# Fused attention, gated MLP and routed experts: turns tied to a place in PE's order, four weight slabs loaded early, the last expert's sums tile by tile, and a re-ordered last routing step

## The chip, the cores and the metric

One NeuronCore of one Trainium2 chip. The metric is device time in microseconds of one execution; the time before is 820.84 us, the median of three runs (818.26 to 821.02). All data are float32 in the reference. The kernel works in the chip's 32-bit matmul type with operands split into a high and a low part, and takes three products for each product of the reference.

## The reference, cut to what matters

```python
def reference(**kwargs):
    attn_out = _attn_ref(**attn_kwargs)              # 2 x 8 heads x 768 x 64, window 96, 8 global
    x = attn_out.transpose(0, 2, 1, 3).reshape(1536, 512)
    x = _moe_ref(x=x, **moe_kwargs)                  # rms norm, (silu(x w_gate) * (x w_val)) w_out, d_ff 1536
    return _moe2_ref(x=x, **moe2_kwargs)

def _moe2_ref(x, w_gate, w_noise, noise, w1, w2):    # 1536 tokens, 512 wide, 8 experts, d_ff 1024
    noisy = x @ w_gate + np.log1p(np.exp(x @ w_noise)) * noise
    top2 = the two largest of noisy per token
    top2_w = softmax over those two
    for e in range(E):
        for k in range(2):
            mask = top2[:, k] == e
            h = np.maximum(x[mask] @ w1[e], 0.0)
            out[mask] += top2_w[mask, k, None] * (h @ w2[e])
```

## The kernel before, in words

The program runs three stages one after another on PE: attention, the gated MLP, and the routed experts. A planner of the framework orders the instructions of each engine: it walks the program with estimated times and issues what it believes to be ready, in program order of priority. `follow(a, b)` (L269) adds an order without a semaphore: a stands behind b on its engine. Each engine then runs its list strictly in that order.

**The MLP** (L1009 to L1058) goes through visits (chunk of hidden blocks, first token tile, number of token tiles). A step f of a visit is `up` for the gate (L646, 12 products), `up` for the value (12 products), `hidden` (tanh, two DVE operations, the split into dh and dl) and the `down` of the step before (L672). The last six visits are of two token tiles each. When a visit of the last chunk ends, its tiles are stored to DRAM as x2d (L685), and `finish` (L999) calls `route` for them.

**Routing** (`route`, L718) transposes two token tiles, evacuates them (L729), forms the logits (L731) in a PSUM bank of tag "o", picks the top two on DVE, counts earlier tokens per expert with small products (L758 to L761), and gets a slot for each choice (sl, L789). The slots, cast to integers (si, L791), drive four scatters on POOL (L812) that write token number and weight into the list metad in DRAM. The two weights come from ed, w1_ (L793 to L800). After the third routing step the fullest expert so far is known (lead); it becomes units 0 and 1, with the first 256 and the other 256 slots of that expert. After the last step, DVE counts and sorts the other seven experts (order, L823 to L830), and SP reads them into registers (value_load, L1059).

**The last routing step** does not go through DRAM for unit 1: `late_slots` (L691) builds four one-hot rows (hot, L700) from sl, multiplies them on PE with late2, which holds a token number and the weight in three bf16 parts (L805 to L807), so that one set of eight products gives token number and weight of each slot. It adds them to the list that was fetched before (L708 to L716), clamps the numbers on POOL (ic, L862), and gathers.

**A unit** (`Unit`, L842) is up to 512 slots of one expert. `slots` fetches its list by an SP transfer (L853) and clamps it; `gather` (L871) brings 128 rows of x2d by an indirect DMA of POOL, 256 KB; `turn` (L881 to L884) transposes the rows on PE into a PSUM bank of tag "t" or "o" and splits them into gh (ACT) and gl (DVE). `run` (L893) goes over eight steps f: `up` (L907, 12 products), Relu and split (zh, zl; L911, L912), and `down` of the step before (L923 or L929). Units 2 to 6 take the transposed form of `down`; units 0, 1, 7 and 8 sum into one bank per tile of 128 slots (L929). After the last step the sums are weighted (L961, L964) and scattered to the output by POOL (L965). Unit 8, the last, has 368 slots, three tiles.

Weights come as slabs of 256 KB by SP (`moe2_weights`, L835 to L841): one w1 and one w2 slab for each f, eight f for each expert, into 19 shared buffers of tag "raw". Units 0 and 1 share theirs. The next unit's slots, gathers, turns and slabs are placed in the program by `side(f)` (L1067) of the unit that runs: fetch at f 0, gathers at f 1 and on, turns at the last f (for unit 1's run, of 4 tiles: f 4 to 7), slabs at each f. SP issues its queue in order.

## Time and profile before

| | before |
|---|---|
| median of 3 runs | 820.84 us (818.26 to 821.02) |
| profiled execution | 815.08 us, of which the span is 812.9 us |
| mean granted TensorE clock | 0.985 |
| PE busy in 420 to 440, 480 to 500, 500 to 520 us | 15.25, 16.74, 14.97 of 20.00 us each |
| DMA moved | 88.76 MB, mean 109 GB/s |

How to read it: the span runs from the first to the last event of the profiled execution. PE is the matmul engine, PEld its weight loads, DVE the vector engine, ACT the scalar engine, POOL the general engine that also issues indirect DMAs, SP the engine that issues the plain ones. A timeline row gives the start, the duration, engine, line, operation, output<-input and, in brackets, the idle time of that engine before it and what ended it. The granted clock is in parts of full speed (1.00 is 2.4 GHz, 0.50 is 1.2 GHz).

### The profile page before, as it was taken

What the parts mean: (1) busy time and instruction counts of PE and PEld (TensorE: products, weight loads), DVE (VectorE), ACT (ScalarE), POOL (GpSimd) and SP (SyncE); (2) the same over time, 40 slices, a digit from 0 to 9 for tenths busy, and PEclk for the clock granted to TensorE, in tenths of its full rate; (3) what the DMA queues carried; (4) which work ended last, traced back from release to release, by engine and by line L of the source; (5) the groups of instructions that cost most, each with busy time, mean ns of one, the idle gap of its engine ahead of it and who ended that gap; (6) DMA issues with size and microseconds to landing.
All of it is one profiled execution on the core that took longest, in us unless ns stands there. A gap on an engine that the chain in (4) does not pass through costs nothing. (4 is left out here: it accounts for less than half of the span.)

```text
span 812.9 us, 13827 instructions
## 1 busy us (share of the span) xinstructions
PE 778.2 (96%) x5041; PEld 696.2 (86%) x5041; DVE 459.6 (57%) x1053; ACT 362.6 (45%) x807; POOL 312.9 (38%) x353
## 2 busy tenths in 40 slices
PE   8999999999899999999997996999999999999993
PEld 5789999999788888899996985888999999999982
DVE  4489866667487887334453575533545454545541
ACT  5677656656443443123332463433333434344430
POOL 7437742232285565002421335342424343524311
PEclk9999999999999999999999999999999999999997
DMA  8465421260242330010108005973363728272010
GB/s 187 106 165 146 118 65 28 45 190 15 79 130 93 118 100 0 1 52 27 27 9 242 25 18 159 330 240 120 104 207 114 246 89 269 87 234 75 36 37 34
DMA packets 116838, 88.76 MB, mean 109 GB/s; under 512 B 49449, under 2 KB 100649, under 8 KB 116768
## 3 DMA queue, kind: packets, MB, share of 16 engines
q1 hardware_dynamic: 107920, 65.43, 28.7%
q0 software_dynamic: 7120, 19.27, 7.1%
q10 hardware_dynamic: 1728, 3.15, 1.3%
q8 instruction: 41, 0.67, 0.4%
q14 instruction: 29, 0.24, 0.1%
HBM read 75.18 MB, written 13.34 MB: 109 GB/s over the span
## 5 line engine op out<-in xcount | busy, mean ns | idle before, releaser
L907 PE MATMUL pz<-gh,sa 128*128 128x256 f32 (+7 forms) x576 | 157.6, 340 | 0.8 <-ACT gh L883 0.8
L907 PEld LDWEIGHTS pz<-gh,sa 128*128 128x128 f32 x576 | 104.2, 190 | 6.2 <-ACT gh L883 1.0
L907 PE MATMUL pz<-gl,sa 128*128 128x256 f32 (+7 forms) x288 | 97.8, 339 | 0.9 <-DVE gl L884 0.9
L672 PE MATMUL acc<-wo,dh 128*128 128x512 f32 x288 | 88.3, 400 | 0.8 <-ACT dh L658 0.8
L923 PE MATMUL ac<-zh,sb 128*128 128x480 f32 (+4 forms) x320 | 86.3, 364 | 0.0
L911 ACT ACTIVATE zh<-pz 128x256 fp32r<-128x256 f32 (+7 forms) x72 | 35.1, 487 | 110.0 <-PE pz L907 110.0
L912 DVE SCALAR_TENSOR_TENSOR zl<-pz,zh 128x256 fp32r<-128x256 f32 (+7 forms) x72 | 39.8, 553 | 75.1 <-ACT zh L911 74.8
L646 PE MATMUL pz<-xTh,wg 128*128 128x256 f32 x352 | 73.7, 288 | 1.2 <-ACT xTh L550 1.0
L646 PE MATMUL pz<-xTh,wv 128*128 128x256 f32 x352 | 73.9, 288 | 0.1
L628 ACT ACTIVATE sa<-wab 128x512 fp32r<-128x512 f32 x72 | 45.2, 629 | 57.9 <-PE ac L923 40.5
L632 DVE TENSOR_TENSOR sa<-wab,sa 128x512 fp32r<-128x512 f32 x51 | 36.6, 720 | 45.5 <-ACT sa L628 45.3
L646 PEld LDWEIGHTS pz<-xTh,wg 128*128 128x128 f32 x352 | 58.4, 192 | 3.5 <-ACT xTh L550 1.2
L923 PEld LDWEIGHTS ac<-zh,sb 128*128 128x128 f32 x320 | 57.9, 188 | 3.2
L672 PEld LDWEIGHTS acc<-wo,dh 128*128 128x128 f32 x288 | 51.3, 189 | 9.7 <-ACT dh L658 1.4
L646 PEld LDWEIGHTS pz<-xTh,wv 128*128 128x128 f32 x352 | 58.4, 192 | 0.8 <-ACT wv L599 0.5
L659 POOL TENSOR_TENSOR dl<-u,dh 128x256 fp32r<-128x256 f32 (+1 forms) x38 | 37.8, 996 | 53.0 <-ACT dh L658 44.7
L907 PEld LDWEIGHTS pz<-gl,sa 128*128 128x128 f32 x288 | 54.8, 190 | 3.8 <-DVE gl L884 1.1
L871 POOL DMA_INDIRECT xg<-x2d,ic x30 | 30.5, 1018 | 67.7 <-PE pg L881 61.3
L812 POOL DMA_INDIRECT metad<-meta,si x24 | 24.3, 1012 | 83.4 <-DVE si L791 77.3
L672 PE MATMUL acc<-wo,dl 128*128 128x512 f32 x144 | 53.0, 400 | 0.2 <-POOL dl L659 0.2
L923 PE MATMUL ac<-zl,sb 128*128 128x480 f32 (+4 forms) x160 | 52.9, 357 | 0.0
L632 DVE TENSOR_TENSOR sb<-wab,sb 128x512 fp32r<-128x512 f32 x67 | 47.1, 703 | 8.9 <-ACT sb L628 8.0
(268 smaller groups left out, 1872.4 us busy)
## 6 DMA issues: line engine op xcount, KB each, us to landing
wab<-in_moe_w_dram SPq DMA_DIRECT2D x128, 256.0 KB, 4.9
rg<-in_moe_w_gate_dram SPq DMA_DIRECT2D x12, 512.0 KB, 3.7
rv<-in_moe_w_val_dram SPq DMA_DIRECT2D x12, 512.0 KB, 3.7
ro<-in_moe_w_out_dram SPq DMA_DIRECT2D x12, 512.0 KB, 3.5
vn<-in_v_dram SPq DMA_DIRECT2D x12, 256.0 KB, 4.4
out_dram<-zero SPq DMA_DIRECT2D x1, 3072.0 KB, 12.8
x2d<-x ACTq DMA_DIRECT2D x12, 256.0 KB, 3.6
kn<-in_k_dram SPq DMA_DIRECT2D x11, 256.0 KB, 3.9
```

Of the source, the lines that this page charges most:

```text
L628: cp = nc.scalar.activation(wp[:, 0], src, AF.Copy)
L632: (nc.gpsimd if pool else nc.vector).tensor_sub(wp[:, 1], src, wp[:, 0].bitcast(F32))
L646: nc.tensor.matmul(pz, a[:, cs], x[:, tt:tt + nt, c, :], start=(n == 0), stop=(n == 3 * DC - 1))
L659: (nc.gpsimd if ci < len(CHUNKS) - 1 else nc.vector).tensor_sub(dl, u, dh.bitcast(F32))
L672: nc.tensor.matmul(acc[t], a[:, tt], w, start=(f == CHUNKS[ci][0] and n == 0), stop=(end and n == 2))
L812: st = nc.gpsimd.indirect_dma_start(out=metad, out_offset=bass.IndirectOffsetOnAxis(ap=si[:, t, kk:kk + 1], axis=0), in_=meta[:, G0[g] + t ...
L871: self.last = nc.gpsimd.indirect_dma_start(out=xg[:m], out_offset=None, in_=x2d[:self.rows], in_offset=bass.IndirectOffsetOnAxis(ap=self.i ...
L907: nc.tensor.matmul(pz[:, :cap], a[:, cs], x[:, c, :cap], start=(k == 0), stop=(k == 3 * DC - 1))
L911: nc.scalar.activation(dh[:, :cap], pz[:, :cap], AF.Relu)
L912: nc.vector.scalar_tensor_tensor(dl[:, :cap], pz[:, :cap], 0.0, dh[:, :cap].bitcast(F32), op0=ALU.max, op1=ALU.subtract)
L923: nc.tensor.matmul(acc[c][:, :cap], w[:, c * P:(c + 1) * P], a[:, :cap], start=(f == 0 and k == 0), stop=(f == FB2 - 1 and k == 2))
```

## The change

- **Turns.** Unit 0's two turns no longer stand in the middle of the visit before the last; each follows, by an order edge, the value products of the last visit's last two steps. Unit 1's two turns follow the eighth `up` of unit 0 (before: program places at f 6 and 7). Unit 2's four turns follow the seventh and eighth `up` of unit 1, two each (before: f 4 to 7, one each).
- **Early weights.** Behind the last routing step SP reads the first expert number alone and loads four of unit 2's eight pairs of slabs there; the rest follow at f 4 to 7 of unit 1's run. The other expert numbers are read one by one, at f 0 of the unit before.
- **Late routing.** `late_slots` is called as soon as sl is there. The one-hot rows are multiplied with the token-number column alone, the sum is clamped on DVE and the gathers are issued; si, ed and the running totals are ordered behind the one-hot rows; the split of the weights is ordered behind the written token numbers, and a second set of eight products then collects the weights. The second tile's transposes are evacuated by DVE. The third `up` of unit 0 is ordered behind the logits.
- **The last expert.** In unit 8 the last two `down` steps are held and done tile by tile, each tile's products in one chain of order edges; the third tile is summed in two halves of 256 columns, in two banks, in all steps, and weighted in two halves.

```diff
@@ -643,8 +643,9 @@
             for a, x in ((wh, xTh[g]), (wh, xTl[g]), (wl, xTh[g])):
-                nc.tensor.matmul(pz, a[:, cs], x[:, tt:tt + nt, c, :], start=(n == 0), stop=(n == 3 * DC - 1))
+                mm = nc.tensor.matmul(pz, a[:, cs], x[:, tt:tt + nt, c, :], start=(n == 0), stop=(n == 3 * DC - 1))
                 n += 1
+        return mm.ins
 
@@ -694,26 +695,33 @@
         h4 = pools["b"].tile([P, GS[-1], 2, 2 * P], BF16, name="hot", tag="raw", bufs=NRAW["b"])
+        idf = sb.tile([P, ns], F32, name="idf")
+        nc.vector.tensor_copy(idf, u.me[:, :ns, 0])
         hot = []
...
                 hot.append((h4[:, t, kk], late2[:, t, kk]))
-        idf = sb.tile([P, ns], F32, name="idf")
-        follow(nc.vector.tensor_copy(idf, u.me[:, :ns, 0]).ins, mark.ins)
         pl = lg[:, 256:256 + 4 * ns].rearrange("p (s c) -> p s c", s=ns)
-        for s in range(ns):
-            for i, (h, m) in enumerate(hot):
-                nc.tensor.matmul(pl[:, s], h[:, s * P:(s + 1) * P], m, start=(i == 0), stop=(i == len(hot) - 1))
+
+        def collect(cols):
+            for s in range(ns):
+                for i, (h, m) in enumerate(hot):
+                    nc.tensor.matmul(pl[:, s, cols], h[:, s * P:(s + 1) * P], m[:, cols], start=(i == 0), stop=(i == len(hot) - 1))
+        collect(slice(0, 1))
         nc.vector.tensor_add(idf, idf, pl[:, :, 0])
-        nc.vector.tensor_copy(u.me[:, :ns, 0], idf)
-        u.slots()
+        u.slots(idf)
         for s in range(ns):
             u.gather(s)
-        mf = u.me.bitcast(F32)
-        gain = sb.tile([P, ns], F32, name="gain")
-        nc.vector.tensor_reduce(gain, pl[:, :, 1:], axis=AX.X, op=ALU.add)
-        nc.vector.tensor_add(mf[:, :ns, 1], mf[:, :ns, 1], gain)
+        found = nc.vector.tensor_copy(u.me[:, :ns, 0], idf).ins
+
+        def gains():
+            collect(slice(1, 4))
+            mf = u.me.bitcast(F32)
+            gain = sb.tile([P, ns], F32, name="gain")
+            nc.vector.tensor_reduce(gain, pl[:, :, 1:], axis=AX.X, op=ALU.add)
+            nc.vector.tensor_add(mf[:, :ns, 1], mf[:, :ns, 1], gain)
+        return mark.ins, found, gains
 
@@ -726,10 +734,13 @@
             xt = sb.tile([P, DC, P], F32, name=f"x2T{ti}", tag="n2", bufs=N2)
-            nc.scalar.activation(xt, p3, AF.Copy)
+            if last and t % 2:
+                nc.vector.tensor_copy(xt, p3)
+            else:
+                nc.scalar.activation(xt, p3, AF.Copy)
             for c in range(DC):
-                nc.tensor.matmul(lg[:, t * 2 * E:(t + 1) * 2 * E], xt[:, c, :], wr[:, c, :], start=(c == 0),
-                                 stop=(c == DC - 1))
+                state["logits"] = nc.tensor.matmul(lg[:, t * 2 * E:(t + 1) * 2 * E], xt[:, c, :], wr[:, c, :], start=(c == 0),
+                                 stop=(c == DC - 1)).ins
         l4 = lg[:, :GT * 2 * E].rearrange("p (t e) -> p t e", t=GT)
@@ -759,8 +770,11 @@
             nc.tensor.matmul(pf[:, t], ones, selsum, start=False, stop=True)
-        for t in range(GT):
-            nc.vector.tensor_add(selsum, selsum, sel[:, t])
+        def total():
+            for t in range(GT):
+                nc.vector.tensor_add(selsum, selsum, sel[:, t])
+        if not last:
+            total()
         pe = small("pe", [E])
@@ -787,12 +801,18 @@
         nc.vector.tensor_reduce(sl.rearrange("p t k -> p (t k)"), oe.rearrange("p t k e -> p (t k) e"), axis=AX.X, op=ALU.add)
+        if last:
+            mark, found, gains = late_slots(sl, lg)
         si = small("si", [2], I32)
-        nc.vector.tensor_copy(si, sl)
+        cast = nc.vector.tensor_copy(si, sl).ins
         ed = small("ed", [1])
-        nc.vector.tensor_sub(ed, m8[:, :, 1:2], m8[:, :, 0:1])
+        w1_ = small("w1_", [1])
+        dif = nc.vector.tensor_sub(ed, m8[:, :, 1:2], m8[:, :, 0:1]).ins
+        if last:
+            follow(cast, mark)
+            follow(dif, mark)
+            total()
         nc.scalar.activation(ed, ed, AF.Exp)
-        w1_ = small("w1_", [1])
         nc.vector.tensor_scalar(w1_, ed, 1.0, 1e-9, op0=ALU.add, op1=ALU.add)
@@ -802,11 +822,13 @@
             for x in range(1, 4):
-                nc.vector.tensor_copy(late2[:, :, :, x], src)
+                part = nc.vector.tensor_copy(late2[:, :, :, x], src)
+                if x == 1:
+                    follow(part.ins, found)
                 if x < 3:
...
                 src = rest
-            late_slots(sl, lg)
+            gains()
         for t in range(GT):
@@ -853,13 +875,16 @@
 
-        def slots(self):
+        def slots(self, ids=None):
             n, ns = self.n, len(self.tiles)
...
             ic = sb.tile([P, NS], I32, name=f"ic{n}", tag="ic", bufs=3)
-            nc.gpsimd.tensor_scalar(ic[:, :ns], me[:, :ns, 0], self.rows - 1, None, op0=ALU.min)
+            if ids is not None:
+                nc.vector.tensor_scalar(ic[:, :ns], ids, float(self.rows - 1), None, op0=ALU.min)
+            else:
+                nc.gpsimd.tensor_scalar(ic[:, :ns], me[:, :ns, 0], self.rows - 1, None, op0=ALU.min)
             self.ic = ic
@@ -872,13 +897,15 @@
 
-        def turn(self, s):
+        def turn(self, s, behind=None):
             m = self.tiles[s][1]
...
             for c in range(DC):
-                nc.tensor.transpose(p3[:, c, :], xg[:m, c * P:(c + 1) * P], ident[:m, :m])
+                mm = nc.tensor.transpose(p3[:, c, :], xg[:m, c * P:(c + 1) * P], ident[:m, :m])
+                if behind is not None:
+                    follow(mm.ins, behind)
             ss = slice(s * P, s * P + m)
@@ -892,9 +919,14 @@
             n, cap, gh, gl = self.n, self.cap, self.gh, self.gl
+            ending = n == E and len(self.tiles) < 4
+
+            def cuts(s):
+
+                return (slice(0, DM // 2), slice(DM // 2, DM)) if ending and s + 1 == len(self.tiles) else (slice(0, DM),)
             wide = cap % P > 0 and cap > 2 * P and n < 8
             acc = [ps.tile([P, 512], F32, name=f"ac{n}_{s}", tag=("d", "d", "t2", "s")[s], bufs=(2, 2, 1, 1)[s])
-                   for s in range(DC if wide else len(self.tiles))]
+                   for s in range(DC if wide else len(self.tiles) + ending)]
             self.ys = {}
@@ -904,8 +936,11 @@
                     for a, x in ((wh, gh), (wh, gl), (wl, gh)):
-                        nc.tensor.matmul(pz[:, :cap], a[:, cs], x[:, c, :cap], start=(k == 0), stop=(k == 3 * DC - 1))
+                        mm = nc.tensor.matmul(pz[:, :cap], a[:, cs], x[:, c, :cap], start=(k == 0), stop=(k == 3 * DC - 1))
+                        if n == 0 and f == 2:
+                            follow(mm.ins, state["logits"])
                         k += 1
+                self.mark = mm.ins
                 dh = pools["b"].tile([P, CAP], F32R, name=f"zh{n}_{f}", tag="dh", bufs=2)
@@ -913,22 +948,42 @@
 
+            def products(f, d, ws, s, x, behind=None):
+                wh, wl = ws
+                m = self.tiles[s][1]
+                o = acc[s + x][:m, cuts(s)[x]]
+                for k, (a, w) in enumerate(((d[0], wh), (d[0], wl), (d[1], wh))):
+                    mm = nc.tensor.matmul(o, a[:, s * P:s * P + m], w[:, cuts(s)[x]], start=(f == 0 and k == 0),
+                                          stop=(f == FB2 - 1 and k == 2)).ins
+                    if behind is not None:
+                        follow(mm, behind)
+                        behind = mm
+                return mm
+
             def down(f, d):
-                wh, wl = split(f"b{self.wkey}_{f}", n)
+                ws = wh, wl = split(f"b{self.wkey}_{f}", n)
                 if n:
                     give(f"ab{self.wkey}_{f}")
+                if ending and f >= FB2 - 2:
+                    held.append((f, d, ws))
+                    if len(held) == 2:
+                        end = len(self.tiles) - 1
+                        turns = [(h, s, 0) for h in held for s in range(end)] + [(h, end, x) for x in range(2) for h in held]
+                        mm = None
+                        for h, s, x in turns:
+                            mm = products(*h, s, x, mm)
+                    return
                 if wide:
...
                     return
-                for s, m in self.tiles:
-                    ss = slice(s * P, s * P + m)
-                    for k, (a, w) in enumerate(((d[0], wh), (d[0], wl), (d[1], wh))):
-                        nc.tensor.matmul(acc[s][:m], a[:, ss], w, start=(f == 0 and k == 0),
-                                         stop=(f == FB2 - 1 and k == 2))
-
+                for s, _ in self.tiles:
+                    for x in range(len(cuts(s))):
+                        products(f, d, ws, s, x)
+
+            held = []
             prev = None
@@ -958,7 +1013,9 @@
                     y = self.ys.pop(s)
-                    nc.vector.scalar_tensor_tensor(y[:m], acc[s][:m], mf[:m, s, 1:2], y[:m], op0=ALU.mult, op1=ALU.add)
+                    for x, cols in enumerate(cuts(s)):
+                        nc.vector.scalar_tensor_tensor(y[:m, cols], acc[s + x][:m, cols], mf[:m, s, 1:2], y[:m, cols],
+                                                       op0=ALU.mult, op1=ALU.add)
                 else:
@@ -1035,7 +1092,7 @@
             side()
-            up(f, "v", t0, nt, pv)
+            vm = up(f, "v", t0, nt, pv)
             d = hidden(ci, f, t0, nt, pg, pv)
@@ -1047,17 +1104,24 @@
                 units[0].gather(1)
-            if kx in (3, 4):
-                units[0].turn(kx - 3)
+            if (ci, t0) == VISITS[-1][:2] and f in CHUNKS[ci][-2:]:
+                units[0].turn(f - CHUNKS[ci][-2], vm)
             if kx is not None and kx < FB2 - 2:
...
 
+    AHEAD = 4
+
+    def name(u):
+        u.e = nc.sync.value_load(order.bitcast(I32)[:1, u.n - 2:u.n - 1], min_val=0, max_val=E - 1)
+
     def late():
...
         for i in range(E - 1):
-            r = nc.sync.value_load(order.bitcast(I32)[:1, i:i + 1], min_val=0, max_val=E - 1)
-            units.append(Unit(2 + i, 1 + i, r, 0, CAPS[i]))
+            units.append(Unit(2 + i, 1 + i, None, 0, CAPS[i]))
+        name(units[2])
+        for f2 in range(AHEAD):
+            moe2_weights(1, units[2].e, f2)
     late()
@@ -1068,12 +1132,22 @@
                     if f == 0:
+                        if nxt.e is None:
+                            name(nxt)
                         nxt.slots()
...
                         nxt.gather(f - 1)
-                if 8 - len(nxt.tiles) <= f:
+                if i == 1:
+                    for s in range(len(nxt.tiles)):
+                        if f == 6 + s // 2:
+                            nxt.turn(s, u.mark)
+                elif i == 0:
+                    if f == FB2 - 1:
+                        for s in range(len(nxt.tiles)):
+                            nxt.turn(s, u.mark)
+                elif 8 - len(nxt.tiles) <= f:
                     nxt.turn(f - 8 + len(nxt.tiles))
-            if nw is not None:
+            if nw is not None and (i > 1 or f >= AHEAD):
                 moe2_weights(nw.wkey, nw.e, f)
...
     fast.close()
```

## Rows read from the trace of the kernel before

**Rows 1.** The page, part 1: busy us (share of the span) xinstructions of each engine.

```profile
PE 778.2 (96%) x5041; PEld 696.2 (86%) x5041; DVE 459.6 (57%) x1053; ACT 362.6 (45%) x807; POOL 312.9 (38%) x353
```

**Rows 2.** Waits of PE, whole span: us in total, times, longest.

```profile
PE pg L881 <- DMA xg<-x2d,ic: 11.5, 3, 5.1
```

**Rows 3.** Windows: length, busy PE, PEld, DVE, ACT, POOL, clock, DMA share, GB/s.

```profile
435.20:444.00 8.80, 3.66 (x16) 3.43 (x16) 1.05 (x2) 0.98 (x2) 0.95 (x2) 0.81 0.99 317
487.90:499.00 11.10, 8.15 (x43) 7.18 (x43) 6.25 (x16) 4.15 (x8) 6.00 (x7) 0.85 0.26 87
503.80:512.10 8.30, 3.27 (x11) 2.76 (x11) 1.85 (x4) 1.50 (x3) 3.17 (x3) 0.79 1.03 335
364.00:370.00 6.00, 6.00 (x39) 5.96 (x39) 0.00 (x0) 0.77 (x2) 0.00 (x0) 0.72 0.00 0
```

**Rows 4.** Timeline at unit 0's start: start, us, engine, line, operation, tiles.

```profile
460.73 0.28 PE L907 MATMUL pz<-gh,sa 128*128 128x256 f32 x1
460.85 0.28 PE L907 MATMUL pz<-gl,sa 128*128 128x256 f32 x1
...
461.50 0.42 DVE L659 TENSOR_TENSOR dl<-u,dh 128x256 fp32r<-128x256 f32 x1 [0.48 <-ACT dh L658]
```

**Rows 5.** Timeline of units 1 and 2: PE and POOL around the gathers.

```profile
485.33 1.36 POOL L871 DMA_INDIRECT xg<-x2d,ic  x1 [0.66 <-POOL ic L862]
...
486.41 0.86 PE L929 MATMUL ac<-sb,zh 128*128 128x512 f32 x3
...
489.23 0.63 PE L881 MATMUL pg<-ident,xg 128*128 128x128 f32 x4 [1.28 <-DMA xg<-x2d,ic]
...
492.18 0.98 POOL L812 DMA_INDIRECT metad<-meta,si  x1 [0.31 <-issue]
...
501.96 1.07 POOL L871 DMA_INDIRECT xg<-x2d,ic  x1 [0.47 <-POOL ic L862]
...
506.65 0.93 POOL L871 DMA_INDIRECT xg<-x2d,ic  x1 [0.30 <-issue]
...
508.89 1.09 PE L881 MATMUL pg<-ident,xg 128*128 128x128 f32 x4 [5.03 <-DMA xg<-x2d,ic]
```

**Rows 6.** Timeline of DVE in the last routing step.

```profile
474.89 1.16 DVE L793 TENSOR_TENSOR ed<-m 128x2 f32<-128x2 f32 x1
...
477.83 1.27 DVE L807 TENSOR_TENSOR rest<-meta,late 128x4 f32<-128x4 f32 x1
...
479.69 0.17 DVE L766 TENSOR_SCALAR ov<-lg 128x16 f32<-128x16 f32 x1
...
483.45 0.15 DVE L708 TENSOR_TENSOR idf<-idf,lg 128x2 f32<-128x2 f32 x1
...
488.23 0.16 DVE L830 FIND_INDEX8 order<-c,cnt 128x8 uint32<-128x8 f32 x1
```

**Rows 7.** Timeline of SP's queue: fetches of a list (L853), loads (L840).

```profile
471.18 27.69 SPq L853 DMA_DIRECT2D me<-metad  x2
...
510.36 2.82 SPq L840 DMA_DIRECT2D wab<-in_moe_w_dram  x1
```

**Rows 8.** Issue to landing, source views: scatter L812, fetch L853, gather L871.

```profile
DMA to landing us min/median/max: 3.2/6.3/7.9
DMA to landing us min/median/max: 1.8/2.1/5.4
DMA to landing us min/median/max: 2.5/4.7/8.0
```

**Rows 9.** Timeline of the end: PE, DVE, POOL.

```profile
796.59 1.55 PE L929 MATMUL ac<-sb,zh 128*128 128x512 f32 x6
...
798.40 2.07 DVE L961 SCALAR_TENSOR_TENSOR y<-ac,me,y 128x512 f32<-128x512 f32 x3 [2.64 <-PE ac L929]
...
799.43 1.01 POOL L965 DMA_INDIRECT out_dram<-y,me  x1 [22.01 <-DVE y L961]
...
802.05 0.96 POOL L965 DMA_INDIRECT out_dram<-y,me  x1 [0.30 <-issue]
```

## The prediction

> **What bounds the kernel now.** I read the page first: PE is busy 778.2 of 812.9 us [rows 1], so time can come only from PE's gaps, from a slower TensorE clock, or from the tail behind PE's last product. The waits of PE come second: three waits on gathered rows (the transposes of a turn, L881) add up to 11.5 us [rows 2]. Third, the windows around them [rows 3]. In 435.2 to 444.0 PE is busy 3.66 of 8.80 us (5.14 idle), in 487.9 to 499.0 it is busy 8.15 of 11.10 (2.95 idle), in 503.8 to 512.1 3.27 of 8.30 (5.03 idle): 13.1 us. The same rows show a second cost: the mean granted clock is 0.81, 0.85 and 0.79, because products behind the idle time run at the lower level, 1.2 GHz instead of 2.4. Lost time is length by missing share: 8.80 x 0.19 = 1.7, 11.10 x 0.15 = 1.7, 8.30 x 0.21 = 1.7, together 5.1 us. So 18.2 us are in reach around the turns of units 0, 1 and 2; the turns of the later units wait for nothing [rows 2].
>
> The profiled execution took 815.08 us (span 812.9), 5.8 less than the median 820.84 of the three runs. I make the sum in microseconds of the profiled one and take it off the median.
>
> **Unit 0's turns** move behind the value products of the last two f steps. Before, the first one sat in PE's order ahead of its rows; they landed inside the first window of [rows 3]. Now PE has about two more f steps to do first, 24 products of 0.12 and 6 of 0.23 or 4.3 us each. Removed: 5.14 + 1.7 = 6.8. New cost: before, unit 0's first product ran at 460.73, ahead of the lower half dl of the last hidden block, which DVE made from 461.50 to 461.92 [rows 4]. Now that product needs the second turn's gh and gl, so PE has little to do until about 461.9. I take 0.5 us, with bounds 0 (the planner finds cover) and 1.4 (a whole first up is pushed out: 12 products at 0.12, the distance of two 256-column products in [rows 4]). The transposes themselves are only moved. Net 6.3.
>
> **Unit 1: token numbers first, weights of the sum behind.** The gather is issued at 485.33, PE ends unit 0's last up at about 486.4, and the first rows are there at 489.23 [rows 5]. The chain in front of the gather is on DVE [rows 6]. Taken out of it: the subtraction for ed, which held DVE for 1.16 us at 474.89: 1.0. The splitting of the weights, its dearest piece 1.27 us at 477.83, ahead of ov at 479.69: 1.4. From the end of the sum (483.60) to the gather 1.73 us pass, with a cast and POOL's clamp between; one DVE instruction of 0.15 and a hand-over of 0.7 stay: 0.8. The second tile's evacuation on DVE has no row here: 0 to 0.7, taken as 0. That is 3.2; other work of DVE may fill part of the room, so I take 2.9 us of lead, bounds 0 and 5. Added are eight narrow products and a copy that stands ahead of the one-hot rows. The first rows then land at 489.2 - 2.9 = 486.3, as PE wants them; the second gather is issued 1.36 + 0.31 = 1.7 later and lands about 488.0, so PE may wait up to 1.2. Both turns stand behind the last up, with two downs (12 products of 0.23, 2.8 us) left to hide gh and gl. The second turn also needs the bank of the logits, which the deferred weights read out: inside the same 1.2. Removed 2.95 + 1.7, residual 0.6 (bounds 0 and 6.2, see B): net 4.1. The scatters of the token list stay behind the gathers on POOL, so they go earlier by the same lead, and their cast si, now behind the one-hot rows, is covered by two gathers. The fresh order edge (unit 0's third up behind the logits) costs nothing while unit 0's two ups and first down, 4.2 us, cover the logits' transposes; without that cover about 1, inside the bounds.
>
> **Unit 2: early weights, turns behind the seventh and eighth up.** Before, SP fetched unit 2's list at 498.9 (the second of the pair that spans 27.69 us from 471.18), then issued 16 weight loads up to 510.36 [rows 7]. The first gather, issued at 501.96, was waited for until 508.89, 6.9 us; the fourth was issued at 506.65 [rows 5], so it landed near 513.6, with the lead 510.7. PE's need: unit 1 starts at 486.4 + 2.8 (two downs) + 0.7 (eight transposes) = 489.9; an f step is 12 x 0.12 + 6 x 0.23 = 2.8; tiles 0 and 1 are turned after the seventh up, 489.9 + 6 x 2.8 + 1.4 = 508.1, and tile 1 (issued at 501.96 + 1.07 + 0.3) lands at 507.3; tiles 2 and 3 follow the eighth up, near 511.5. The slack is 0.8. Half of the loads now go ahead of the fetch: eight at (510.36 - 498.9) / 16 = 0.7, about 6 us of SP behind the value load of the order. Behind them stands the fetch; its cover is the landing of the last scatter, from 493.2 [rows 5] to 498.9. Removed 5.03 + 1.7, residual 0.6 taken, bounds 0 and the whole 6.7: net 6.1. The row shows a gather that needs 6.9 us under a backlog of loads, against 2.5 at the least [rows 8]. The Trainium skill, DMA: Bandwidth & Descriptors, section Queues, rings and completion order, says that each DMA engine serves its queue rows in turn, a packet at a time; by it a gather of 256 KB would get half of the 335 GB/s, 1.6 us on top of 2.5, an estimate of 4.1, the residual would be 0 and the sum 18.1 instead of 17.5. The measured 6.9 decides.
>
> The other six value loads go from the wait on the order to one per unit. Seven of them fit between the order (488.4 [rows 6]) and 498.9, so each takes at most 1.5; nothing, as no turn of the later units waits.
>
> **The end.** Six products took 1.55 us from 796.59, 0.23 each; three more end at 798.8. All tiles end together: DVE starts at 798.40, scatters are issued from 799.43 to 802.05, 1.3 apart [rows 9]. Tile by tile, three whole and twelve half products stand behind the first tile's last: 0.7 + 1.4 = 2.1 us. DVE starts near 796.9, the scatters near 797.9, 799.2 and 800.5; the last tile's second half is ready near 799.7. Gain 1.5, bounds 0 (what follows the last scatter up to 812.9 is not shown) and 2.1. Six held products (1.4 us) cover the making of the last hidden block. Price on PE: 24 products become 48 halves; at 0.12 against 0.23 that is 0.2, at most 5.5 if a half cost a whole, which [rows 4] speak against. With the eight narrow products: 0.4 (0.3 to 1.2).
>
> **Sum:** 6.3 + 4.1 + 6.1 + 1.5 - 0.4 = 17.6, taken as 17.5: 815.1 becomes 797.6 in a like execution, the median 820.8 becomes 803.3.
>
> **Rivals.** A, *unit 2 still waits*, because the early loads meet the scatters and the fetch. Landing goes up to 7.9 for a scatter and 5.4 for a fetch [rows 8], against 5.7 and at most 3.1 here: 4.5 later, less the slack 3.7 of idle, plus 1.7 of clock. Sum 17.5 + 0.6 - 5.4 = 12.7: 808.1. The Trainium skill, Trainium Kernel Development and Optimization, section Key Constraints, says that transfers of all issuing engines run on the same 16 engines and interleave, which is this. For it: DMA share 1.03 in that window. Against: the loads now start in a quiet one, share 0.26 [rows 3].
> B, *no lead for unit 1*: DVE's free time is filled by other work, both turns stand ahead of the downs, and PE waits until 490.9: 4.5 us and 1.7, 6.2 instead of 0.6. Sum 11.9: 808.9.
> C, *the waits only move*: B, unit 2's wait whole, 1.4 instead of 0.5 at unit 0, and one clock drop of 1.7 without idle, as in 364 to 370, where PE is never idle and the clock 0.72 [rows 3]: 17.5 - 5.6 - 6.1 - 0.9 - 1.7 = 3.2: 817.6, no change.
> D, *slower: the order comes late*. Its count and sort stand behind deferred sums on DVE, and on PE the count's product may be planned behind turns that wait for rows; SP stands then, with eight loads and unit 2's fetch behind it. The last rows are there 6 + 3.1 + 4.7 + 6.9 = 20.7 us after the order, against a need at 511.5. An order 19 us later than at 488.4 eats the whole gain; 24 us later gives about 826. Against: the count and sort are some ten short DVE instructions.
>
> **Chances.** Forecast 0.63, A 0.13, B 0.11, C 0.07, D 0.06. 0.5% is 4.1 us, about what a measurement of this kernel can tell from no change: faster by more 0.87 (forecast, A, B), within it 0.07 (C), slower 0.06 (D). Range 799.5 to 812: below, no residuals and a little of the 2.8 us that the runs differ by; above, A or B with 3 us of their bounds. C and D are left out.
>
> **What would show it.** After: no wait of PE on gathered rows over 1.5 us in units 0 to 2; granted clock 1.00 through the three stretches; unit 2's fetch behind eight loads and within 14 us of unit 1's gather, as now; the last scatter about 1.5 us behind the last half. It is wrong if L881's successor still waits over 4 us in all, if the clock drops beside the grouped transposes, or if unit 1's gather stands no earlier against unit 0's last up.

## The result, and the profile after

Four runs each: 819.74 us before (818.26 to 821.02) and 806.48 us after (804.86 to 808.06), ratio 0.9839, 95% interval 0.981 to 0.9868. That is 13.3 us less where 17.5 were forecast; the range held it. The profiled execution after took 806.28 us (span 804.5, clock 0.992), against 815.08 before: only 8.8 less, half the forecast. Two later sets of runs on other chips gave 11.0 and 10.5 us.

The page, part 1, of the kernel after; its line answers to [rows 1]:

```profile
PE 774.6 (96%) x5073; PEld 693.0 (86%) x5073; DVE 460.3 (57%) x1056; ACT 362.3 (45%) x806; POOL 312.7 (39%) x352
```

PE's busy time fell by 3.6 us, although 32 instructions more are recorded: a product at the lower clock counts as longer busy time, and the mean clock rose from 0.985 to 0.992. The waits of PE from 430 to 530 us, after (us in total, times, longest), answer to [rows 2]:

```profile
PE pz L939 <- DVE sa L632: 2.5, 1, 2.5
PE pz L939 <- DVE gl L911: 2.5, 2, 2.1
PE pz L939 <- ACT gh L910: 1.9, 2, 1.2
PE pg L906 <- DMA xg<-x2d,ic: 0.7, 1, 0.7
PE acc L673 <- ACT dh L659: 0.5, 1, 0.5
```

The 11.5 us on gathered rows became 0.7, as forecast. What was not forecast stands above it: 2.5 us on a weight half that DVE splits, and 4.4 us on gl and gh, where 1.7 stood before. All idle time of the stretch is 8.1 us, against 13.1 before. The windows of [rows 3] again, with one that holds the clock:

```profile
435.20:444.00 8.80, 8.80 (x68) 8.30 (x67) 5.93 (x10) 4.25 (x9) 3.38 (x4) 1.00 1.02 330
503.80:512.10 8.30, 8.30 (x56) 7.47 (x55) 5.38 (x10) 4.54 (x10) 4.44 (x6) 1.00 1.11 335
490.00:498.00 8.00, 6.28 (x34) 6.02 (x35) 4.63 (x11) 2.27 (x5) 2.27 (x2) 0.79 0.65 187
```

The first and the last of the old holes are full at clock 1.00. One drop is left, 8.00 x 0.21 = 1.7 us, behind the waits at unit 1. These are they, and the wait while unit 0 runs, in PE's timeline:

```profile
456.71 0.40 PE L939 MATMUL pz<-gh,sa 128*128 128x256 f32 x2
...
469.77 0.50 PE L939 MATMUL pz<-gh,sa 128*128 128x256 f32 x2 [2.52 <-DVE sa L632]
...
484.07 0.41 PE L906 MATMUL pg<-ident,xg 128*128 128x128 f32 x2 [0.66 <-DMA xg<-x2d,ic]
...
489.14 0.50 PE L939 MATMUL pz<-gh,sa 128*128 128x256 f32 x2 [1.18 <-ACT gh L910]
491.72 0.38 PE L939 MATMUL pz<-gl,sa 128*128 128x256 f32 x1 [2.08 <-DVE gl L911]
```

Before, the 2.95 us of unit 1's hole were not all for rows either. Of them 1.28 were ([rows 5]), and the rest stood here, in PE's timeline before:

```profile
492.45 0.50 PE L907 MATMUL pz<-gh,sa 128*128 128x256 f32 x2 [0.77 <-ACT gh L883]
493.85 0.39 PE L907 MATMUL pz<-gl,sa 128*128 128x256 f32 x1 [0.90 <-DVE gl L884]
```

After the change, the rest of the idle time, 0.77 and 0.42 us (and 0.46 at unit 0's start), stands at unit 2's first products, for gh and gl of its last tiles. DVE's timeline says where the 2.52 us come from:

```profile
468.94 0.17 DVE L699 CAST idf<-me 128x2 f32<-128x2 int32 x1 [6.86 <-DMA me<-metad]
469.02 0.69 DVE L632 TENSOR_TENSOR sa<-wab,sa 128x512 fp32r<-128x512 f32 x1
469.63 0.17 DVE L752 TENSOR_TENSOR ny<-ny,nz 128x16 f32<-128x16 f32 x1
...
472.55 1.01 DVE L775 TENSOR_TENSOR selsum<-selsum,sel 128x8 bf16<-128x8 bf16 x1
...
489.60 0.73 DVE L1021 TENSOR_SCALAR y<-ac,me 128x512 f32<-128x512 f32 x1
...
490.32 0.74 DVE L1021 TENSOR_SCALAR y<-ac,me 128x512 f32<-128x512 f32 x1
490.98 0.68 DVE L911 TENSOR_TENSOR gl<-pg,gh 128x512 fp32r<-128x512 f32 x1
```

The copy idf<-me, now ahead of the one-hot rows, reads unit 1's token list. DVE takes its instructions in order, so it stood 6.86 us at this 0.17 us copy, until a DMA had brought the list. Behind the copy stood the weight split that PE waited for and the first step of the routing chain. At 489.60, two results of unit 0 (0.73 and 0.74 us) run ahead of the gl that PE waits for.

Unit 2's gathers, on POOL, and the end:

```profile
502.70 0.78 POOL L887 TENSOR_SCALAR ic<-me 128x4 int32<-128x4 int32 x1 [9.52 <-DMA me<-metad]
503.75 1.07 POOL L896 DMA_INDIRECT xg<-x2d,ic  x1 [0.28 <-POOL ic L887]
...
790.94 1.01 POOL L1022 DMA_INDIRECT out_dram<-y,me  x1 [20.39 <-DVE y L1017]
...
793.56 0.96 POOL L1022 DMA_INDIRECT out_dram<-y,me  x1 [0.30 <-issue]
```

The last scatter starts 10.9 us before the end of the span, as before ([rows 9]: 812.9 - 802.05). It stands 1.6 us nearer to PE's last product.

**How executions are compared below.** The program in front of the last MLP visits is the same in both kernels, yet it took other times in other executions: the same product, behind a wait of 0.3 us near 415, starts at 414.66 us before and at 415.99 after. So beside the medians I read a stretch free of that: from the first up of unit 0 (456.71 above; S) to the end of the span. After: 804.45 - 456.71 = 347.7. S itself lies at 456.71, 455.58 and 453.48 in three executions of the changed kernel, so what stands in front of it moves by 3.2 us without any change. The order of products around S differs in the kernel before, so its stretch is read from run 5 below, which adds unit 0's part alone: 351.2.

### The profile page after: what moved, and what is told of

Its sections match the earlier page's. It is cut to its first block, busy times and chain, and to the rows that moved or that the text cites. A ratio compares the mean times of both kernels' runs of the same rounds, so it can differ in the third digit from the quotient of the medians.

```text
span 804.5 us, 13883 instructions
## 1 busy us (share of the span) xinstructions
PE 774.6 (96%) x5073; PEld 693.0 (86%) x5073; DVE 460.3 (57%) x1056; ACT 362.3 (45%) x806; POOL 312.7 (39%) x352
## 5 line engine op out<-in xcount | busy, mean ns | idle before, releaser
L646 PE MATMUL pz<-xTh,wv 128*128 128x256 f32 x352 | 72.2, 284 | 0.0
```

The source lines that it names most:

```text
L646: mm = nc.tensor.matmul(pz, a[:, cs], x[:, tt:tt + nt, c, :], start=(n == 0), stop=(n == 3 * DC - 1))
```

## The experiments

Times are medians of 5 or 6 runs. Runs 1 to 4 shared a chip (before: 817.19), so did 5 to 8 (815.66) and 9 to 11 (815.00); run 12 had 814.75 beside it. In runs with edits above them, the changed kernel's lines move by up to 23.

```
run                        us       ratio to before       S to the end
1  changed kernel          806.17   0.9874 0.9851-0.9897  347.6
2  copy behind             802.99   0.9835 0.9809-0.9860  344.8
3  + count first, y late   802.77   0.9822 0.9803-0.9842  343.4
4  no early loads          803.89   0.9842 0.9814-0.9869  346.6
5  before + unit 0 alone   807.53   0.9903 0.9878-0.9927  351.2
6  old turns of unit 2     806.03   0.9881 0.9857-0.9905  348.0
7  old end                 806.80   0.9889 0.9859-0.9919  349.8
8  3 without early loads   806.15   0.9886 0.9859-0.9912  347.1
9  changed kernel          804.52   0.9887 0.9865-0.9908  348.5
10 old routing             801.56   0.9849 0.9824-0.9875  345.0
11 8 + list buffer, pins   802.06   0.9840 0.9820-0.9860  343.6
12 10 without early loads  806.62   0.9903 0.9880-0.9927  349.0
```

**Runs 1 and 9: the changed kernel again.**

> The changed kernel itself, once more, so that the other three runs have it beside them. If the waits are the kernel's own: a wait of PE near 2.5 us for a weight half that DVE splits (L632) while unit 0 runs, one near 2.1 us for gl of unit 1's second turn (L911), one clock drop right behind it, and a ratio of 0.984 against the kernel before. If they were one execution's chance: other waits in other places, and a ratio outside 0.981 to 0.987.

> The changed kernel once more, beside the two runs of this call. Theory (its margin at unit 2 is under 3 us, so whatever PE wins at unit 1 it waits at unit 2): waits at unit 1 for gh and gl and at unit 2 for rows that together come to 4 to 6 us, however they are split, and 806 us as before. Rival (unit 2's wait is gone for good, and what is left is unit 1's): no wait over 0.5 us for unit 2's rows, 3 to 4 us for gh and gl.

Run 1 waited 1.9 us for the weight half, 3.2 for gl, 1.1 for gh, so the waits are the kernel's own. Its ratio, 0.9874, still lies above the 0.984 that was expected and just outside the bounds named for chance: the kernel before was faster on this chip (817.19, not 819.74). Run 9, in PE's timeline:

```profile
465.91 0.51 PE L939 MATMUL pz<-gh,sa 128*128 128x256 f32 x2 [1.88 <-DVE sa L632]
...
485.15 0.50 PE L939 MATMUL pz<-gh,sa 128*128 128x256 f32 x2 [0.22 <-ACT gh L910]
...
486.87 0.39 PE L939 MATMUL pz<-gl,sa 128*128 128x256 f32 x1 [1.22 <-DVE gl L911]
...
506.53 0.63 PE L906 MATMUL pg<-ident,xg 128*128 128x128 f32 x4 [2.31 <-DMA xg<-x2d,ic]
```

Unit 1 waits less here, so PE comes to unit 2 earlier, and now waits 2.31 us for its rows, with a clock drop behind it (clock 0.72 in 506 to 512). The waits at units 1 and 2 add up to 5.1 us either way (run 9 with 0.76 and 0.63 at unit 2's start; 5.1 in the first execution, 0.66 + 1.18 + 2.08 + 0.77 + 0.42; 5.5 in run 1, with 1.18 us at unit 1 for which the profile names no cause). The theory of run 9 holds, its rival falls. Unit 2's wait was only covered by unit 1's.

**Run 2: the copy behind the one-hot rows again.** PE's order is the same.

```diff
-        idf = sb.tile([P, ns], F32, name="idf")
-        nc.vector.tensor_copy(idf, u.me[:, :ns, 0])
...
+        idf = sb.tile([P, ns], F32, name="idf")
+        follow(nc.vector.tensor_copy(idf, u.me[:, :ns, 0]).ins, mark.ins)
```

> The copy idf<-me goes behind the one-hot rows again; nothing else moves, PE's order is the same. Theory (a copy that waits for a DMA holds DVE's queue): the wait of 2.52 us on sa and the copy's own 6.86 us in front of it are gone, the routing chain starts 3 us earlier, unit 1's first rows are there before PE wants them (0.66 us of wait gone), and the time falls by 2.5 to 4.5 us against the changed kernel, to about 803. Rival 1 (the chain was late anyway, the copy merely stands where the wait was): the wait on sa is as long for another reason and the time changes by under 0.8 us. Rival 2 (an earlier list of tokens makes the scatters and the fetch of unit 2 meet other transfers): the wait on sa goes, but the time does not fall.

The waits of PE from 430 to 530, of run 2:

```profile
PE pz L939 <- DVE gl L911: 2.4, 2, 1.9
PE pz L939 <- ACT gh L910: 1.6, 2, 0.9
PE acc L673 <- ACT dh L659: 0.5, 1, 0.5
PE lg L769 <- DVE sel L766: 0.3, 1, 0.3
PE pg L906 <- DMA xg<-x2d,ic: 0.2, 1, 0.2
PE ac L956 <- ACT zh L946: 0.2, 1, 0.2
```

The wait on sa is gone, and the wait for unit 1's rows (the 0.2 is unit 2's). 806.17 became 802.99, 3.2 us, and S to the end 2.8 less than in run 1: the theory, inside its bounds; both rivals fall. The size is loose, since two of the five runs (805.50 and 806.38) lie among run 1's.

**Run 3: the count's product ahead of unit 1's transposes, unit 0's results behind the second gl**, on top of run 2.

```diff
+                if self.n == 1:
+                    follow(mm.ins, state["count"])
...
+                    if n == 0:
+                        follow(scaled.ins, units[1].cut)
```

> As the run before, and two orders more: the count's product on PE stands ahead of unit 1's transposes, and unit 0's two results on DVE (L1021, 0.74 us each) stand behind the lower half gl of unit 1's second turn. Theory (gl of the second turn is late because its bank is freed late and DVE does other work first): the 1.18 and 2.08 us that PE waits for gh and gl shrink to about 1.2 together, and with them the clock drop of 1.7 us goes; 3 to 4 us less than the run before, near 799.5. Rival (the clock drop belongs to the grouped transposes, not to the idle time): the waits shrink by 2, the drop stays, 1.5 to 2.5 us less. Rival (unit 1's first down waits for the banks that unit 0's results still hold): a new wait of 1 to 1.5 us on the first product of ac, under 1 us won.

The wait for gh and gl at unit 1 became 0.43 and 0.45 us, behind a new one of 0.69 us of the second turn for the count's copy (482.25). No clock drop follows (clock 1.00 in 482 to 492), so the drop is not the grouped transposes'. But the next wait grew, in PE's timeline:

```profile
484.72 0.50 PE L941 MATMUL pz<-gh,sa 128*128 128x256 f32 x2 [0.43 <-ACT gh L912]
...
485.67 0.39 PE L941 MATMUL pz<-gl,sa 128*128 128x256 f32 x1 [0.45 <-DVE gl L913]
...
505.61 0.63 PE L906 MATMUL pg<-ident,xg 128*128 128x128 f32 x4 [1.42 <-DMA xg<-x2d,ic]
```

Of 3 to 4 us expected, 1.4 came in S to the end and 0.2 in the median. It ran 803.00 at most, run 1 805.03 at least.

**Run 4: no early loads.**

```diff
-    AHEAD = 4
+    AHEAD = 0
```

> The changed kernel without the eight early weight loads of unit 2: its list is fetched right behind the order, and all sixteen loads follow the fetch. Theory E (the early loads took unit 2's wait away, since they leave less in front of its gathers): PE waits 3 to 5 us for unit 2's rows again and the clock drops, 4.5 to 6.7 us more than the changed kernel. Theory L (the later turns did it): the fetch goes about 6 us earlier, the gathers too, even 6.9 us of landing end before the turns at 510, and the time is within 1 us of the changed kernel's.

Theory L on the time: nothing lost. The median is 2.3 us lower, S to the end 1.0; its runs (801.92 to 807.03) overlap run 1's. POOL's timeline of run 4 at unit 2's gathers:

```profile
495.00 0.69 POOL L887 TENSOR_SCALAR ic<-me 128x4 int32<-128x4 int32 x1 [2.32 <-DMA me<-metad]
495.97 1.07 POOL L896 DMA_INDIRECT xg<-x2d,ic  x1 [0.28 <-POOL ic L887]
```

From S (455.44) the first gather is issued at 40.5 us; after, at 503.75 - 456.71 = 47.0; in run 5, with the old routing and loads, at 493.56 - 453.62 = 39.9. So the change did not bring unit 2's gathers forward. It pushed them back by 7 us, and without the early loads they are nearly where they were, and unit 2 waits for no row. But the loads do it only together with the new routing: run 10, with early loads and the old routing, issues the gather at 41.0 (494.55 - 453.55), and run 12, with neither, at 37.2. So the loads cost 6.5 us with the new routing and 3.8 with the old, and the routing 6.0 with the loads and 3.3 without.

**Run 5: unit 0's turns alone**, in the kernel before (the diff's parts for `up`, `turn` and the loop over the visits).

> The kernel before with one part of the change alone: unit 0's two turns behind the value products of the last two f steps. Theory (the part is worth what its stretch lost, and it keeps it): PE's wait of 5.14 us near 435 and the clock drop behind it are gone, some 0.5 us of wait stand at unit 0's start instead, the waits of units 1 and 2 stay (about 3 and 5 us), and the time falls by 6.3 us against the kernel before. Rival (given back later): unit 1's chain or unit 2's gathers do not move with PE, their waits grow by what was won, and under 2 us are left.

8.1 us in the median, 6.3 expected. The profile gives 6.4: 5.14 idle and 1.7 of clock gone, 0.46 come. A new wait of 1.04 us for a weight half in unit 0's run took back what units 1 and 2 waited less. The other 1.7 us of the median have no account. The window that held 5.14 us of idle time is full:

```profile
435.20:444.00 8.80, 8.80 (x71) 8.38 (x69) 5.60 (x10) 3.95 (x8) 1.38 (x1) 1.00 0.91 308
```

Units 1 and 2 wait 0.82 and 4.45 us for rows: not given back. This one part carries most of what the whole change won.

**Run 6: unit 2's turns in their old places**, early loads kept (the branch `if i == 1` taken out).

> The changed kernel with unit 2's four turns where they were (one per f step from the fifth on), the eight early loads kept. Theory L (the later turns took unit 2's wait away): PE waits 2 to 4 us for unit 2's rows and the clock drops by 1.7 more, 3 to 6 us above the changed kernel. Theory E (early loads and an earlier token list are enough): PE waits under 0.8 us for them, the waits of 0.77 and 0.5 us for gh and gl shrink, and the time is within 1 us of the changed kernel's or a little under it.

PE waits 3.17 us for unit 2's rows, where run 9 waits 2.31 and run 7, with the later turns too, 2.92. The time is the changed kernel's. Without the wait the first turn would come 505.58 - 456.21 = 49.4 us after S, in run 9 504.22 - 453.48 = 50.7: the new place moved PE's need by 1.4 us, not by two f steps. Neither theory as it stood: the wait is there, but the later turns hardly shorten it.

**Run 7: the old end** (`ending = False`).

> The changed kernel with the old end: all tiles of the last expert end together. Theory (the tail is worth what the first tiles' results run ahead): from PE's last product to the end of the span 14.1 us instead of 12.5, PE ends 0.2 earlier, 1.5 us more in all (0 to 2.1). Rival (the end hangs on what follows the last transfer, not on the transfers): the tail stays at 12.5 to 13, within 0.5 us.

POOL's timeline of its end:

```profile
789.80 1.01 POOL L1022 DMA_INDIRECT out_dram<-y,me  x1 [22.01 <-DVE y L1017]
...
792.42 0.96 POOL L1022 DMA_INDIRECT out_dram<-y,me  x1 [0.31 <-issue]
```

PE ends at 789.19, the span at 803.31: 14.1 us, as before, against 12.5 after. The last scatter is again 10.9 us ahead of the end, so the rival falls. The theory holds in the profile; in the time the 1.5 us are inside the interval.

**Runs 8 and 11: run 3 without early loads, then with a fourth list buffer and every later turn behind its up.**

```diff
-    AHEAD = 4
+    AHEAD = 0
...
-            me = sb.tile([P, NS, 2], I32, name=f"me{n}", tag="me", bufs=3)
+            me = sb.tile([P, NS, 2], I32, name=f"me{n}", tag="me", bufs=4)
...
-                    nxt.turn(f - 8 + len(nxt.tiles))
+                    nxt.turn(f - 8 + len(nxt.tiles), u.mark)
```

> The run with the copy behind, the count first and unit 0's results late, and now without the eight early loads. Theory (the early loads only push unit 2's fetch and gathers back): the gathers go 4 to 6 us earlier against unit 1's first turn, the 1.4 us that PE waited for unit 2's rows and the 0.8 and 0.9 us for gh and gl are gone, and it takes 1.5 to 3 us less than with them, near 800.5. Rival (the scatters' landing holds the fetch anyway, so nothing is won): the fetch stands within 1 us of where it was, same time.

> The run without early loads, with two things more: a fourth buffer for the token lists (32 bytes a partition), so that unit 3's fetch does not wait until unit 0's result scatter has landed, and every later unit's turns behind the up product of their step. Theory (the wait of 7.15 us for unit 3's rows came from a list buffer held by unit 0's late result scatter): the fetch of unit 3 follows unit 2's last load within 1 us instead of 4.2, no wait over 1 us from unit 1 to unit 3, no clock drop between 470 and 530, and it takes 7 to 10 us less than that run, near 797. Rival (the queue of transfers holds unit 3's rows, not the buffer): the fetch is earlier, PE still waits 3 to 7 us for unit 3's rows, and under 4 us are won.

Run 8 reached unit 2 without a wait over 0.4 us, its first gather 37.0 us after S against 42.8 in run 3, and then stood at unit 3's rows. So both fall, the theory on the time (806.15, not 800.5; S to the end 3.7 us longer than in run 3) and the rival on the fetch (31.9 us after S, 35.6 in run 3):

```profile
513.99 1.09 PE L906 MATMUL pg<-ident,xg 128*128 128x128 f32 x4 [7.15 <-DMA xg<-x2d,ic]
```

With the fourth buffer (run 11) the fetch of unit 3 follows the last load of unit 2 by 0.8 us instead of 4.2, but its list lands no earlier, and now the loss has another name; PE's and POOL's timelines of run 11:

```profile
514.39 1.17 PE L941 MATMUL pz<-gh,sa 128*128 128x480 f32 x2 [3.97 <-POOL sa L632]
```

```profile
509.96 0.23 POOL L887 TENSOR_SCALAR ic<-me 128x4 int32<-128x4 int32 x1 [10.10 <-DMA me<-metad]
```

POOL's clamp waits 10.10 us for the list, and a weight split that PE needs stands behind it: run 2's mechanism on another engine. The buffer theory falls for the time: 802.06, not 797. Of the rival, the earlier fetch holds and that the list gains nothing by it (it comes 506.75 - 453.34 = 53.4 and 509.96 - 456.62 = 53.3 us after S); the wait it named, on unit 3's rows, is not there. What the two edits did apart was not tried. Run 11 still lies under run 9 on the same chip (803.56 at most, against 804.02 at least).

**Run 10: the late routing as before** (`late_slots` and `route` of the kernel before, with the edge behind the logits kept).

> The changed kernel with the late routing as it was before (weights and token numbers in one product, the copy behind the one-hot rows, one evacuation engine); turns, early loads and end as changed. Theory (the new order of the routing gave unit 1 nothing): unit 1 waits 1 to 1.5 us for rows and 1.6 for gh and gl, no 1.9 us for a weight half, and the time lies within 1.5 us of the changed kernel's, rather under it. Rival (the lead is worth what was forecast): unit 1's first rows come 2 to 3 us later against PE, the scatters and unit 2's fetch too, and it takes 3 to 4.5 us more.

3.0 us less than the changed kernel beside it, 3.5 in S to the end. Its waits from 430 to 530:

```profile
PE pg L883 <- DMA xg<-x2d,ic: 2.0, 2, 1.6
PE lg L708 <- DVE hot L701: 1.0, 1, 1.0
PE acc L673 <- ACT dh L659: 0.5, 1, 0.5
PE lg L759 <- DVE sel L756: 0.4, 1, 0.4
```

The 2.0 are unit 2's; unit 1 waits for nothing. So the theory was right on the side and short on the size: the new routing costs about 3 us (two of the six runs, 805.04 and 805.47, lie among run 9's). Unit 1's first gather shows how, in us from S: 23.5 in run 5 (477.07 - 453.62), 20.9 here (474.45 - 453.55) and in run 12, 19.4 in run 2 (478.29 - 458.85), 19.3 to 19.4 in runs 3, 8 and 11, and 22.6 in run 9 (476.05 - 453.48; 22.0 and 21.4 in the two executions before it). The old routing with the edge behind the logits is 2.6 ahead of run 5, which has no edge; the new order brings 1.5 more where the copy does not wait; the waiting copy takes 2.0 to 3.2 back. Of the 2.6, the logits' products make 1.4: they end 7.9 us after S with the edge, 9.3 without. The rest I did not follow. DVE's lines, then POOL's, of run 10 show why the new order saved so little:

```profile
464.18 1.16 DVE L794 TENSOR_TENSOR ed<-m 128x2 f32<-128x2 f32 x1
...
467.12 1.27 DVE L806 CAST late<-meta 128x4 bf16<-128x4 f32 x1
```

```profile
464.03 1.29 POOL L632 TENSOR_TENSOR sb<-wab,sb 128x512 fp32r<-128x512 f32 x1 [4.70 <-ACT sb L628]
466.97 1.39 POOL L632 TENSOR_TENSOR sb<-wab,sb 128x512 fp32r<-128x512 f32 x1 [1.65 <-ACT sb L628]
```

The long DVE instructions end within 0.04 us of POOL's splits (465.34 and 465.32; 468.39 and 468.36). It is so before, too: the two of [rows 6] end at 476.05 and 479.10, and POOL's splits at 476.04 and 479.09. In POOL's timeline before:

```profile
474.75 1.29 POOL L632 TENSOR_TENSOR sb<-wab,sb 128x512 fp32r<-128x512 f32 x1 [3.39 <-ACT sb L628]
477.68 1.41 POOL L632 TENSOR_TENSOR sb<-wab,sb 128x512 fp32r<-128x512 f32 x1 [1.65 <-ACT sb L628]
```

So their length is POOL's. In the kernel after, ed took 0.15 us, started in the same 0.01 us as a split (475.32), and that split took 1.91 us instead of 1.3. There the one that met a running split was selsum (1.01 us at 472.55, the split from 472.24 to 473.54). Not every small instruction waits: ov and pe, each with an input in PSUM, took 0.17 us inside the same split.

**Run 12: run 10 without early loads.**

> The run with the old routing, now without the eight early loads too: unit 0's and unit 2's later turns, the edge behind the logits and the tile-by-tile end are all that is left of the change. Theory (the early loads run into the scatters of the token list and hold the fetch behind them): from the last scatter's issue to the fetch of unit 2 it takes some 4 us instead of 9, its gathers stand 3 to 5 us earlier against unit 1, the 1.6 and 0.4 us of PE's wait for unit 2's rows and the clock drop behind them are gone, and the ratio to the kernel before is 0.980 to 0.982. Rival 1 (the scatters land that late by themselves): the fetch stands where it was, ratio 0.985. Rival 2 (without loads ahead, unit 3's list or a weight half comes late): a new wait of 3 us or more in unit 2's first f steps, ratio 0.985 or above.

The gathers do come earlier (493.28 - 456.12 = 37.2 us after S, 41.0 in run 10) and unit 2's wait is gone; from the last scatter to the fetch it takes about 5.6 us instead of 9.0. But rival 2 decides:

```profile
518.09 1.08 PE L883 MATMUL pg<-ident,xg 128*128 128x128 f32 x4 [6.23 <-DMA xg<-x2d,ic]
```

These are unit 3's rows. The early loads buy something after all: SP issues eight loads before unit 2's fetch, so that it reaches unit 3's fetch sooner (46.3 us after S in run 10, 51.4 here; 2.4 of the difference is the list buffer, held by unit 0's result scatter).

Below the changed kernel's median on the same chip lie runs 2, 3 and 4 (by 3.2, 3.4 and 2.3 us) and runs 10 and 11 (3.0 and 2.5); all runs of 3 and of 11 lie below all of the changed kernel's beside them.

## Why the prediction was right, and where not

The sign and the range held, on all chips; the forecast of 17.5 was too large. In the first profiled pair, in us:

```
term      forecast  measured
unit 0      6.3       6.4    5.14 + 1.7 - 0.46
unit 1      4.1      -3.5    2.95 + 1.7 - 2.52 - 0.66 - 1.18 - 2.08 - 1.7
unit 2      6.1       5.5    5.03 + 1.7 - 0.77 - 0.42
end         1.5       1.6    14.13 - 12.49
PE more    -0.4      -0.2    remainder
in front     -       -1.3    415.99 - 414.66, not of the change
sum        17.6       8.5    the spans: 812.9 - 804.5
```

By its own signs the prediction was half right. No wait on rows passed 1.5 us in the first execution, but 2.31 in run 9; the clock was 1.00 in two of the three stretches and 0.85 in unit 1's (487.9 to 499.0); unit 2's fetch came 496.15 - 478.74 = 17.4 us behind unit 1's first gather, not within 14. The median, 806.48, lies nearer to the rivals A (808.1) and B (808.9) than to the 803.3 of the forecast. That it lies inside the range is owed to the range, which was drawn to take in A or B, and not to unit 1's term.

**Right:** unit 0's term, to 0.1 us in the profile, with its residual of 0.5 (run 5 has it alone, with 8.1 us in the median); the end, in the profile; that the turns of the later units wait for nothing.

**Wrong: unit 1's term, at three places.** "Added are eight narrow products and a copy that stands ahead of the one-hot rows": the copy was counted as an instruction and not as a wait. Its source is a list that a DMA brings, and I did not ask what is queued behind it. Run 2 prices that at about 3 us. "Inside the same 1.2" for the second turn: its bank was freed by the count's copy, planned behind the first turn, and its gl stood behind two results on DVE; 3.3 us in the first execution, 1.4 in run 9, 0.9 with both orders mended (run 3), beside the 0.69 for the count's copy. Against that, the 1.7 us for gh and gl that were there before were part of the 2.95 and counted as gone. And the lead of 3.2 took the 1.16 and 1.27 us of [rows 6] for the price of two instructions; they were POOL's, and the measured lead of the new order is 20.9 - 19.4 = 1.5. Rival B's loss at unit 1 came in size (3.9 us of waits and 1.7 of clock, where B had 4.5 and 1.7), more for gh and gl than for rows; the first turn stood ahead of both downs, as B has it, the second ahead of their last two products only. The Trainium skill, SBUF — State Buffer, section Who interferes with whom, has the rule: a DVE instruction with two SBUF inputs contends with a GpSimd one that reads SBUF, and whoever is second waits for the whole instruction. The ends of ed, rest and selsum agree, to 0.02 us, and so does the split that took 1.91 us beside ed; the cast of run 10 has one SBUF input, and this sentence does not cover it.

**Missed:** the edge behind the logits was costed at nothing. The logits end 1.4 us earlier in run 10, which has it, than in run 5, and unit 1 waits for no row even with the old routing. Run 10 also has unit 1's later turns and the early loads, so the edge's own share is not shown.

**Right by luck: unit 2's term.** The slack was put at 0.8 us. In the first execution the rows were in time because PE had lost 4 us at unit 1; in run 9 PE loses 1.4 there and 2.3 here. What the early loads were to do, they do not do for unit 2 (run 4). Rival A named them as the cause, and part of it is real: the list is fetched behind eight loads and lands about 6 us later. (The estimate of 4.1 us for a gather adds a whole transfer to 2.5 us that hold one already; nothing hangs on it.) Rival C, that the waits only move, describes runs 3, 8, 11 and 12. Of D a small part came true: the order is ready 484.47 - 461.36 = 23.1 us behind the logits in run 9 and 17.0 in run 10, 6 us later, not the 19 at which D decides. With it unit 2's first gather stands 45.9 us after S in run 9, 41.0 in run 10.

What stays open: why the same program in front of unit 0 differs between executions and chips, and so why the gain over the kernel before was 13.3, 11.0 and 10.5 us. Nor was it tried alone which of the copy, the deferred sums and the count makes D's 6 us. The order starts 32.8 us after S in run 1, 29.6 in run 2, 28.9 in run 3, 26.7 in run 8 and 24.9 in run 10, so the waiting copy is some 3 us of it.

## What to carry to other kernels

An instruction moved ahead in an in-order queue brings its wait with it: before it is called free, name what brings its operands, and what stands behind it (shown by run 2 on DVE; on POOL, in run 11, read off the rows). A wait removed on a chain with 1 us of slack comes back at the next turn, so ask for each stage when its transfers are issued and not only when they are needed. A tiny instruction that takes seven times its usual time is not dear; look which instruction of another engine it ends with.

## What was not expected of the hardware

- Small DVE instructions (128x2 and 128x4 elements) took 1.16 and 1.27 us beside a split on POOL, and 0.15 to 0.17 us elsewhere. Started together with the split, ed kept its 0.15 us and the split took 1.91 instead of 1.3.
- From the last scatter's issue to the end of the span it took 10.9 us in the profiles of both kernels and of all twelve runs, with the old end and with the new, so the end of the span moved with the last scatter.
- Most clock drops here cost 1.7 us (0.21 x 8.00 in 464 to 472 and 0.28 x 6.00 in 506 to 512 of run 9). Behind the long waits of runs 8 and 12 the missing share comes to 3.4 and 3.5 us (0.14 x 24.00 in 506 to 530; 0.16 x 22.00 in 508 to 530), part of it while PE stood idle anyway. Not every wait draws a drop: the same 1.88 us in unit 0's run drew one in run 9 and none in runs 6 and 7 (clock 1.00), 1.01 in run 10 did, and 2.52 in the first execution after did not.
